# Splitting each mid-run K and V load into two half-row loads on two DMA queues

## The chip, the cores and the metric

The kernel runs on one core of a Trainium2 chip. The metric is the device time of one execution in microseconds (us). A core has a matrix engine (PE), a vector engine (VectorE, DVE in the profile), a scalar engine (ScalarE, ACT), GpSimd (POOL) and SyncE (SP), which only issues transfers, and 16 DMA engines that move data between the main memory (HBM) and the on-chip memory. Each engine runs its own list of instructions in order; they wait for each other by semaphores. A transfer is issued by an engine onto that engine's own DMA queue, and the 16 DMA engines work the queues off.

## The reference, cut to what matters

One decoding step of attention over a cache of 8192 positions, for 2 tokens (batch B = 2) and 32 heads of width 128, and a small MLP whose result gates the attention output. All arrays are float32.

```python
def _A_ref(x, k_cache, v_cache, wq, wo):      # x: 2 x 1 x 512, caches: 2 x 32 x 8192 x 128
    q = (x @ wq).reshape(B, Sq, H, Dh).transpose(0, 2, 1, 3)
    scores = jnp.einsum("bhqd,bhkd->bhqk", q, k_cache) * (Dh ** -0.5)
    p = softmax(scores, axis=-1)
    o = jnp.einsum("bhqk,bhkd->bhqd", p, v_cache)
    return o.transpose(0, 2, 1, 3).reshape(B, Sq, H * Dh) @ wo
def _B_ref(x, w1, b1, w2, b2):                # 512 -> 1376 -> 512
    return gelu(layernorm(x) @ w1 + b1) @ w2 + b2
xn = layernorm(A_x)
return A_x + _A_ref(xn, ...) * silu(_B_ref(xn, ...))
```

Every byte of the K and V caches (2 x 268 MB) has to be read once, and nearly all of the kernel's traffic is that.

## The kernel before, in words

The 64 (token, head) rows are handled two at a time, as N = 32 pairs. For one pair the 2 x 8192 keys lie over the 128 partitions, 64 partitions to a head, so that each partition holds 128 keys of 128 numbers: 16384 floats, 64 KB, in one row that is also contiguous in HBM. K of a pair is therefore one transfer of 128 rows of 64 KB (8.39 MB), and so is V. On the chip there are three such buffers: two for K (`kb0`, `kb1`, the K of alternate pairs) and one for V (`vb`).

What is done for pair n:

- VectorE multiplies K by the query in place, one half of the rows' length at a time (`scores_mul`, L523; half s = 0 is the first 64 keys of each partition, s = 1 the other 64), then sums each product (`scores_sum`, L530, again one instruction per half) and takes the maximum (L534), which PE turns (L537) and VectorE reduces (L540).
- In the next pair's time PE spreads the maximum (L546), ScalarE copies it (L547), takes the exponentials (L551) and scales a selector row (L555); this is `exps`.
- `weighted` is the product of the weights with V: 32 matmuls of 512 columns on PE (L574; the profile counts each as two instructions, hence x64), which read V from its first to its last column; ScalarE copies the result out (L581), PE folds it (L583) and VectorE places it (`spread`, L589).

The order is written out by hand. In the iteration of pair n VectorE runs mul(n, 0), the reduction of pair n-1, mul(n, 1), sum(n, 0), sum(n, 1), max(n) and spread(n-1); `exps` and `weighted` of pair n-1 lie beside them. `load_v(n)` is issued after `weighted(n-1)`, which frees `vb`; `load_k(n+2)` after the sums of pair n, which free that K buffer. All loads are issued by SyncE through `load` (L314), so they are on one queue in the order of the program. K of the first and of the last pair (n = 0 and 31) are already two loads of half a row each, both from SyncE; V of the last pair goes into `kb1` in the same way; then come five pieces of the output weights `wo` into `vb`.

`Plan` records every operation with the tiles that it reads and writes, and derives the waits from that: a load of a buffer waits for the last reader of it. In `emit` each engine's instructions come out in recorded order. Operations with `loop=True` (the middle pairs on PE, VectorE and ScalarE) are put into a hardware loop, for which each turn must have the same waits and the same signals; `HEADS` places the loop's head in the instruction buffer. SyncE has no loop: its loads are written out one by one. A PE instruction raises its semaphore only if somebody waits for it (`tell`).

Of the kernel before, what the change touches and what calls it, by code (L numbers as in the profile page):

```python
# [11 lines left out]

HEADS = {"pe": 0, "dve": 160, "act": 128}


class Op:
# [3 lines left out]
class Plan:  # L22
# [18 lines left out]
    def op(self, eng, fn, r=(), w=(), over=(), it=None, loop=False, dma=None):  # L41


        o = Op()
        o.eng, o.fn, o.it, o.loop, o.dma, o.tell = eng, fn, it, loop, dma, False
        need = {}

        def after(d, war):
            if d.dma is None and dma is None and d.eng == eng and (eng == "pe" or war):
                return  # L50
            if d.dma is None:
                if need.get(d.eng) is None or need[d.eng].idx < d.idx:
                    need[d.eng] = d
            else:
                k = ("dma", d.dma)
                if need.get(k) is None or need[k].idx < d.idx:
                    need[k] = d

        for k in r:
            if k in self.writer:  # L60
                after(self.writer[k], False)
        for k in list(w) + list(over):
            if k in self.writer:
                after(self.writer[k], False)
            for d in self.readers.get(k, ()):
                after(d, True)
        clock = self.clock[eng]
        need = {k: d for k, d in need.items() if clock.get(k, 0) < d.idx}
        o.deps = [(k, d) for k, d in need.items()
                  if not any(e is not d and e.done.get(k, 0) >= d.idx for e in need.values())]  # L70
        for _, d in o.deps:
            for k, v in d.done.items():
                clock[k] = max(clock.get(k, 0), v)
        own = eng if dma is None else ("dma", dma)
        self.count[own] = o.idx = self.count.get(own, 0) + 1
        o.done = dict(clock)
        o.done[own] = o.idx
        for k in w:
            self.writer[k] = o
            self.readers[k] = []  # L80
        for k in r:
            if k not in w:
                self.readers.setdefault(k, []).append(o)
        self.ops.append(o)

    def emit(self, heads):

        nc = self.nc
        for o in self.ops:
            for _, d in o.deps:  # L90
                d.tell = True
        sems, value, told = {}, {}, {}
        for o in self.ops:
            key = o.eng if o.dma is None else ("dma", o.dma)
            if key not in sems:
                sems[key] = nc.alloc_semaphore(o.eng if o.dma is None else f"dma_{o.dma}")

            step = 16 if o.dma is not None else int(o.tell or o.eng != "pe")
            told[key] = told.get(key, 0) + step
            value[id(o)] = told[key]  # L100
        for o in self.ops:
            o.waits = {k: value[id(d)] for k, d in o.deps}

        def put(o, waits, turn=None):
            e = self.eng[o.eng]
            for k, v in waits:
                e.wait_ge(sems[k], v)
            i = o.fn() if o.it is None else o.fn(o.it if turn is None else turn)
            if o.dma is not None:
                i.then_inc(sems[("dma", o.dma)], 16)  # L110
            elif o.tell or o.eng != "pe":
                i.then_inc(sems[o.eng], 1)

        def order(d):
            return sorted(d.items(), key=lambda kv: str(kv[0]))

        for e in self.eng:
            ops = [o for o in self.ops if o.eng == e]
            inside = [j for j, o in enumerate(ops) if o.loop]
            if not inside:  # L120
                for o in ops:
                    put(o, order(o.waits))
                if e == "sp":

                    nc.sync.wait_ge(sems[("dma", "out")], told[("dma", "out")])
                continue
            for o in ops[:inside[0]]:
                put(o, order(o.waits))
            turns = {}
            for j in inside:  # L130
                turns.setdefault(ops[j].it, []).append(ops[j])
            n, m = len(turns), len(turns[1])
            assert inside == list(range(inside[0], inside[-1] + 1)) and list(turns) == list(range(1, n + 1))
            assert all(len(t) == m for t in turns.values())


            body, ahead = [], {}
            for j in range(m):
                col = [turns[i][j] for i in range(1, n + 1)]
                assert len({o.tell for o in col[1:-1]}) == 1, j  # L140
                for o in col:
                    o.tell = col[1].tell
                ws = []
                for k in sorted(set().union(*(o.waits for o in col)), key=str):
                    if all(k not in o.waits for o in col[1:]):
                        ahead[k] = max(ahead.get(k, 0), col[0].waits[k])
                        continue
                    step = col[2].waits[k] - col[1].waits[k]
                    base = col[1].waits[k] - 2 * step
                    for o in col:  # L150
                        assert o.waits.get(k) == step * o.it + base or (o.it == 1 and k not in o.waits), \
                            (e, j, k, o.it, [x.waits.get(k) for x in col])
                    ws.append((k, step, base))
                body.append((col[1], ws))
            for k, v in order(ahead):
                self.eng[e].wait_ge(sems[k], v)
            et = self.eng[e].engine
            with nc.Fori(1, n + 1, 1, engines=bass.OrderedEngineSet([et]), head_slot={et: heads[e]}) as i:
                for o, ws in body:
                    put(o, [(k, i * step + base if base else i * step) for k, step, base in ws], i)  # L160
            for o in ops[inside[-1] + 1:]:
                put(o, order(o.waits))


def decode_kernel(nc, x, kc, vc, wq, wo, w1, b1, w2, b2, out):
# [13 lines left out]
    JW = 512 // DH  # L179
# [17 lines left out]
    op = plan.op  # L197
# [5 lines left out]
        op("dve", fn, r, w, it=it, loop=loop)  # L203

    def act(fn, r=(), w=(), it=None, loop=False):
        op("act", fn, r, w, it=it, loop=loop)

    def pool(fn, r=(), w=()):
        op("pool", fn, r, w)
# [10 lines left out]
    kb = [sbuf(f"kb{i}", [P, KP * DH]) for i in range(2)]  # L220
    vb = sbuf("vb", [P, KP * DH])
    kbuf = [t.rearrange("p (j d) -> p j d", d=DH) for t in kb]
    vbuf = vb.rearrange("p (j d) -> p j d", d=DH)
# [36 lines left out]
    boot = []  # L260
# [49 lines left out]
    vf = vc.rearrange("b h s d -> (b h s d)").rearrange("(n p j d) -> n p j d", p=P, j=KP, d=DH)  # L310
    M = KP // 2

    def load(dst, src, sem, w, over=()):
        op("sp", lambda: nc.sync.dma_start(dst, src), (), w, over=over, dma=sem)  # L314

    def load_k(n):
        i = (n + 1) % 2
        if n in (0, N - 1):
            for s in range(2):
                load(kbuf[i][:, s * M:(s + 1) * M], kf[n][:, s * M:(s + 1) * M], f"k{i}{s}", [("kb", i, s)])  # L320
            return
        load(kbuf[i], kf[n], f"kb{i}", [("kb", i, s) for s in range(2)])


    WO_PIECES = (0, 16, 24, 29, 31, 32)
# [175 lines left out]
    load_k(1)  # L501

    def load_v(n):
        load(vbuf, vf[n], "v", ["vb"], over=boot)

    load_v(0)

# [56 lines left out]
    def weighted(n):  # L564

        one = dict(it=n + 1, loop=n < N - 1)
        last = n == N - 1
        v = kbuf[1] if last else vbuf  # L570
        for t in range(NT):
            j = t % QT
            keys = [("kb", 1, t * JW // M)] if last else ["vb"]
            pe(lambda i, t=t, j=j, v=v: matmul(PO[R * j:R * j + U * JW, :], PZ[:, t].rearrange("p s j -> p (s j)"),  # L574
                                               v[:, t * JW:(t + 1) * JW, :].rearrange("p j d -> p (j d)"),
                                               start=(t < QT), stop=(t + QT >= NT)),
               keys + [("PZ", s) for s in range(U)], ["po"], **one)
        if last:
            busy(1)

        act(lambda i: nc.scalar.copy(O4, PO), ["po"], ["o4"], **one)  # L581
        for k in range(JW):
            pe(lambda i, k=k: matmul(PT[:, :U], O4[:, k * DH:(k + 1) * DH], mod[:, k:U * JW:JW],  # L583
                                     start=(k == 0), stop=(k == JW - 1)), ["o4", "mod"], ["s0"], **one)
# [32 lines left out]

    wo_r = wo.rearrange("(p c) n -> p c n", p=P)
    for i, (a, e) in enumerate(zip(WO_PIECES, WO_PIECES[1:])):
        load(wo_sb[:, a:e], wo_r[:, a:e], f"wo{i}", [("wo", i)], over=["vb"])  # L620

    max_dve(N - 1)
    exps(N - 1)
# [73 lines left out]
```

## Time and profile before

| | |
|---|---|
| Time, median of 3 runs | 1299.54 us (1299.47 to 1299.76) |
| Profiled execution, first to last instruction (span) | 1298.1 us; its own time is given by the span alone, and the median of the runs is 1.4 us above it |
| Busy share of DVE, PE, ACT | 87%, 31%, 6% |
| SyncE's queue q1 | 10936 packets, 559.36 MB, 99.7% of 16 DMA engines' span |
| Mean rate | 431 GB/s |

A packet is one piece that one DMA engine moves. "DMA share" in a table of stretches is the part of the 16 DMA engines' time in which a packet was in work. "SPq" marks the instruction with which SyncE issues a transfer. A row of the timeline gives the start in us, the duration in us, the engine, the line, the operation, output and input, how many, and in brackets the idle time just before and what ended it.

### The profile page before, as it was taken

What the parts mean: (1) busy time and instruction counts of PE and PEld (TensorE: products, weight loads), DVE (VectorE), ACT (ScalarE), POOL (GpSimd) and SP (SyncE); (2) the same over time, 40 slices, a digit from 0 to 9 for tenths busy, and PEclk for the clock granted to TensorE, in tenths of its full rate; (3) what the DMA queues carried; (4) which work ended last, traced back from release to release, by engine and by line L of the source; (5) the groups of instructions that cost most, each with busy time, mean ns of one, the idle gap of its engine ahead of it and who ended that gap; (6) DMA issues with size and microseconds to landing.
All of it is one profiled execution on the core that took longest, in us unless ns stands there. A gap on an engine that the chain in (4) does not pass through costs nothing.

```text
span 1298.1 us, 6788 instructions
## 1 busy us (share of the span) xinstructions
PE 408.0 (31%) x2728; PEld 123.3 (9%) x2728; DVE 1134.3 (87%) x276; ACT 77.7 (6%) x250; POOL 1.4 (0%) x8
## 2 busy tenths in 40 slices
PE   5603333312333312333321333321333321233327
PEld 1200111000101000101100101100001000001102
DVE  2499999988889988889988888988888988888991
ACT  1200000000000000000000000000000000000000
POOL 0000000000000000000000000000000000000000
PEclk9856666556666656666656666656666655666658
DMA  9999999999999999999999999999999999999998
GB/s 404 445 425 442 426 432 440 424 444 428 438 430 426 442 428 440 428 434 438 424 444 428 438 430 426 444 426 440 428 430 442 424 444 428 436 432 426 430 434 365
DMA packets 10943, 559.45 MB, mean 431 GB/s; under 512 B 1220, under 2 KB 1332, under 8 KB 1592
## 3 DMA queue, kind: packets, MB, share of 16 engines
q1 hardware_dynamic: 10936, 559.36, 99.7%
q8 instruction: 4, 0.07, 0.0%
q14 instruction: 3, 0.02, 0.0%
HBM read 559.30 MB, written 0.06 MB: 431 GB/s over the span
## 4 chain that ended last, share of the span: by engine, by line
DMA 68%; PE 24%; DVE 4%; issue 3%; ACT 0%; SPq 0%; DVEq 0%
DMA vb<-in_A_v_cache_dram 65%; PE po L574 21%; DMA vb<-in_A_wo_dram 2%; DVE sc L530 2%; DVE kb L523 1%; PE s L409 1%; DMA vb<-in_A_x_dram 1%; PE po L481 1%; PE s L451 0%; PE s L411 0%; PE acc L656 0%; DVE vb L417 0%; ACT L430 0%; PE s L458 0%; SPq L314 0%
## 5 line engine op out<-in xcount | busy, mean ns | idle before, releaser
L523 DVE TENSOR_TENSOR kb<-kb,Q 128x8192 f32<-128x8192 f32 x64 | 555.5, 8681 | 101.2 <-DMA kb<-in_A_k_cache_dram 91.9
L530 DVE TENSOR_REDUCE sc<-kb 128x64 f32<-128x8192 f32 x64 | 552.3, 8666 | 0.0
L574 PE MATMUL po<-vb,PZ 128*8 128x512 f32 x1984 | 284.4, 738 | 282.9 <-DMA vb<-in_A_v_cache_dram 280.3
L546 PE MATMUL s<-nm,srow 1*128 1x2 f32 x64 | 18.4, 355 | 360.0 <-DVE nm L540 360.0
L574 PEld LDWEIGHTS po<-vb,PZ 128*8 128x8 f32 x1984 | 56.8, 103 | 484.4 <-issue 481.6
L537 PE MATMUL s<-ident,mx 128*1 128x128 f32 x32 | 11.8, 369 | 198.9 <-DVE mx L534 198.9
L546 PEld LDWEIGHTS s<-nm,srow 1*128 1x128 f32 x64 | 15.7, 302 | 369.3 <-DVE nm L540 369.3
L581 ACT COPY o<-po 128x512 f32<-128x512 f32 x32 | 18.7, 585 | 527.5 <-PE po L574 527.5
L547 ACT COPY bias<-s 128x2 f32<-128x2 f32 x32 | 5.1, 160 | 624.0 <-PE s L546 624.0
L583 PE MATMUL s<-mod,o 128*128 128x2 f32 x256 | 33.6, 253 | 22.1 <-ACT o L581 22.1
L583 PEld LDWEIGHTS s<-mod,o 128*128 128x128 f32 x256 | 31.0, 191 | 51.4 <-ACT o L581 51.4
L551 ACT ACTIVATE PZ<-sc,bias 64x128 f32<-64x128 f32 x64 | 25.5, 399 | 1.8
L537 PEld LDWEIGHTS s<-ident,mx 128*1 128x1 f32 x32 | 2.5, 79 | 202.4 <-DVE mx L534 171.9
L589 DVE TENSOR_TENSOR Z<-blk,s 128x8 f32 (+1 forms) x32 | 5.2, 162 | 13.5 <-PE s L583 13.5
L417 DVE COPY vb<-vb 2x384 f32<-2x384 f32 x4 | 1.8, 500 | 15.6 <-ACT vb L413 15.6
L409 PE MATMUL s<-vb 128*2 128x512 f32 (+1 forms) x24 | 12.2, 658 | 0.3 <-ACT vb L374 0.3
L551 ACT ACTIVATION_READ_ACCUMULATOR PZ<-sc,bias 64x1 f32 x64 | 11.8, 185 | 0.0
L665 DVE TENSOR_TENSOR gate<-acc,gate 128x128 f32<-128x128 f32 x1 | 0.3, 291 | 12.1 <-PE acc L656 12.1
L574 PE MATMUL po<-kb,PZ 128*8 128x512 f32 x64 | 9.8, 779 | 1.4 <-ACT PZ L551 1.4
L534 DVE TENSOR_REDUCE mx<-sc 128x1 f32<-128x128 f32 x32 | 9.1, 286 | 1.1
L555 ACT ACTIVATE ZR<-half,rs 128x8 f32 (+1 forms) x32 | 9.6, 301 | 4.1
L540 DVE TENSOR_REDUCE nm<-s 1x2 f32<-1x128 f32 x32 | 8.7, 272 | 0.3 <-PE s L537 0.3
(88 smaller groups left out, 82.9 us busy)
## 6 DMA issues: line engine op xcount, KB each, us to landing
kb<-in_A_k_cache_dram SPq DMA_DIRECT2D x4, 4096.0 KB, 42.8
kb<-in_A_v_cache_dram SPq DMA_DIRECT2D x2, 4096.0 KB, 40.8
vb<-in_B_w_dram SPq DMA_DIRECT2D x2, 2752.0 KB, 12.6
vb<-in_A_wo_dram SPq DMA_DIRECT2D x1, 4096.0 KB, 20.6
vb<-in_A_wo_dram SPq DMA_DIRECT2D x1, 2048.0 KB, 25.1
vb<-in_A_wo_dram SPq DMA_DIRECT2D x1, 1280.0 KB, 27.7
vb<-in_A_wo_dram SPq DMA_DIRECT2D x1, 512.0 KB, 28.5
vb<-in_A_v_cache_dram SPq DMA_DIRECT2D x31, 29.3
```

What stands on the lines that cost most here:

```text
L409: pe(lambda f=f, w=w, ph=ph, c=c: matmul(ph[:B, :w], yT[:, c, :], w1_sb[:, c, f:f + w], start=(c == 0), stop=False), ["yT", "w1"], [k])
L481: pe(lambda i=i, c=c, wv=wv, a=a, j=j, hd=hd: matmul(PO[R * j:R * j + NQ * B, :].rearrange("m (h d) -> m h d", d=DH), xnT[:, c, a:a + NQ * ...
L523: vector(n, n, lambda n: nc.vector.tensor_tensor(out=k, in0=k, in1=cols(Q, n * DH, DH).unsqueeze(1).to_broadcast([P, M, DH]), op=ALU.mult) ...
L530: vector(n, n, lambda n: nc.vector.tensor_reduce(out=SC[:, s * M:(s + 1) * M], in_=k, axis=AX.X, op=ALU.add), [("kb", i, s)], [("sc", s)])
L534: vector(n, n, lambda n: nc.vector.tensor_reduce(out=MX, in_=SC, axis=AX.X, op=ALU.max), [("sc", 0), ("sc", 1)], ["mx"])
L537: pe(lambda i: transpose(PM[:1, :P], MX, ident), ["mx", "ident"], ["s1"], it=n, loop=n > 0)
L546: pe(lambda i: matmul(PN[:, :U], srow, NM, start=True, stop=True), ["srow", "nm"], ["s2"], **one)
L551: act(lambda i, r=r, s=s: nc.scalar.activation(PZ[r, :, s, :], sc[r], AF.Exp, bias=BIAS[r, s:s + 1], scale=SCALE, accum_out=RS[r]), ["bias ...
L555: act(lambda i: nc.scalar.activation(cols(ZR, i * UP - UP, UP), half, AF.Copy, scale=RS), ["half"] + [("rs", s) for s in range(U)], [("ZR" ...
L574: pe(lambda i, t=t, j=j, v=v: matmul(PO[R * j:R * j + U * JW, :], PZ[:, t].rearrange("p s j -> p (s j)"), v[:, t * JW:(t + 1) * JW, :].rea ...
L581: act(lambda i: nc.scalar.copy(O4, PO), ["po"], ["o4"], **one)
L583: pe(lambda i, k=k: matmul(PT[:, :U], O4[:, k * DH:(k + 1) * DH], mod[:, k:U * JW:JW], start=(k == 0), stop=(k == JW - 1)), ["o4", "mod"], ...
```

## The change

K of pairs 1 to 30 and V of pairs 0 to 30 are each loaded by two transfers of 128 rows of 32 KB in place of one of 128 rows of 64 KB. The first half of each row is issued by SyncE, the second by ScalarE (`q="act"`), each on its own queue and with its own semaphore. With that:

- The tile `vb` becomes two tiles, one for each half, so that the matmuls of the first 16 steps of `weighted` wait for SyncE's half alone, the others for ScalarE's; and each half of a buffer is loaded again when its own readers are done, no longer when the readers of the whole are.
- ScalarE's operations leave the hardware loop (`act` no longer hands on `loop`) and are written out one by one, 31 turns, since transfers are now among them. In ScalarE's order the load of V's half comes behind the copy L581, and the load of K's half behind that; the copy L547 of the next pair comes behind both.
- In `emit` the signals of the turns of a loop are made equal (`tell`), since a PE matmul in the middle of `weighted` now has somebody waiting for it.
- K of pairs 0 and 31, V of pair 31 and all other loads stay on SyncE.

```diff
-HEADS = {"pe": 0, "dve": 160, "act": 128}
+HEADS = {"pe": 0, "dve": 160}
...
+        for e in self.eng:
+            turns = {}
+            for o in self.ops:
+                if o.eng == e and o.loop:
+                    turns.setdefault(o.it, []).append(o)
+            for col in zip(*turns.values()):
+                said = any(o.tell for o in col)
+                for o in col:
+                    o.tell = said
...
     def act(fn, r=(), w=(), it=None, loop=False):
-        op("act", fn, r, w, it=it, loop=loop)
+        op("act", fn, r, w, it=it)
...
-    def load(dst, src, sem, w, over=()):
-        op("sp", lambda: nc.sync.dma_start(dst, src), (), w, over=over, dma=sem)
+    queue = {"sp": nc.sync, "act": nc.scalar}
+
+    def load(dst, src, sem, w, over=(), q="sp"):
+        op(q, lambda: queue[q].dma_start(dst, src), (), w, over=over, dma=sem)
...
-        load(kbuf[i], kf[n], f"kb{i}", [("kb", i, s) for s in range(2)])
+        for s, q in enumerate(("sp", "act")):
+            load(kbuf[i][:, s * M:(s + 1) * M], kf[n][:, s * M:(s + 1) * M], f"kb{i}{s}", [("kb", i, s)], q=q)
...
     def load_v(n):
-        load(vbuf, vf[n], "v", ["vb"], over=boot)
+        for s, q in enumerate(("sp", "act")):
+            load(vbuf[:, s * M:(s + 1) * M], vf[n][:, s * M:(s + 1) * M], f"v{s}", [("vb", s)], over=boot, q=q)
...
-            keys = [("kb", 1, t * JW // M)] if last else ["vb"]
+            keys = [("kb", 1, t * JW // M)] if last else [("vb", t * JW // M)]
...
-        load(wo_sb[:, a:e], wo_r[:, a:e], f"wo{i}", [("wo", i)], over=["vb"])
+        load(wo_sb[:, a:e], wo_r[:, a:e], f"wo{i}", [("wo", i)], over=[("vb", s) for s in range(2)])
```

## The prediction

> **What bounds the kernel now.** I read the page first: busy shares, the slices of DMA, the queues. Then the list of transfers.
>
> ```profile
> span 1298.1 us, 6788 instructions
> PE 408.0 (31%) x2728; PEld 123.3 (9%) x2728; DVE 1134.3 (87%) x276; ACT 77.7 (6%) x250; POOL 1.4 (0%) x8
> ...
> DMA  9999999999999999999999999999999999999998
> ...
> DMA packets 10943, 559.45 MB, mean 431 GB/s; under 512 B 1220, under 2 KB 1332, under 8 KB 1592
> ...
> q1 hardware_dynamic: 10936, 559.36, 99.7%
> q8 instruction: 4, 0.07, 0.0%
> q14 instruction: 3, 0.02, 0.0%
> ...
> vb<-in_A_v_cache_dram SPq DMA_DIRECT2D x31, 29.3
> kb<-in_A_k_cache_dram SPq DMA_DIRECT2D x30, 42.5
> ```
>
> The reader is to see that one queue, q1, keeps all 16 DMA engines at work for 99.7% of the span, with no weak slice. VectorE is next at 87%. So the time is the bytes over the rate of the DMA engines, and an edit counts only if it changes that rate, opens a gap in it, or lengthens what follows the last byte. The last two rows count the loads that the change touches: 31 + 30 = 61.
>
> Next, one pair in the middle from the timeline, to see how much hides behind the queue.
>
> ```profile
> 608.15 0.33 SPq L314 DMA_DIRECT2D vb<-in_A_v_cache_dram  x1
> 608.15 0.58 ACT L581 COPY o<-po 128x512 f32<-128x512 f32 x1 [18.00 <-PE po L574]
> 613.66 0.33 SPq L314 DMA_DIRECT2D kb<-in_A_k_cache_dram  x1
> 617.68 8.69 DVE L523 TENSOR_TENSOR kb<-kb,Q 128x8192 f32<-128x8192 f32 x1 [3.64 <-DMA kb<-in_A_k_cache_dram]
> 626.29 0.27 DVE L540 TENSOR_REDUCE nm<-s 1x2 f32<-1x128 f32 x1
> 627.24 0.16 ACT L547 COPY bias<-s 128x2 f32<-128x2 f32 x1 [18.50 <-PE s L546]
> 628.57 0.30 ACT L555 ACTIVATE ZR<-half,rs 128x8 f32 x1
> 635.09 17.26 DVE L530 TENSOR_REDUCE sc<-kb 128x64 f32<-128x8192 f32 x2
> 637.00 9.21 PE L574 MATMUL po<-vb,PZ 128*8 128x512 f32 x64 [9.80 <-DMA vb<-in_A_v_cache_dram]
> 656.36 8.69 DVE L523 TENSOR_TENSOR kb<-kb,Q 128x8192 f32<-128x8192 f32 x1 [3.58 <-DMA kb<-in_A_k_cache_dram]
> 665.17 8.67 DVE L523 TENSOR_TENSOR kb<-kb,Q 128x8192 f32<-128x8192 f32 x1
> ```
>
> Both readers wait for their transfer: VectorE 3.6 us in each pair, PE 9.8 us. A load is issued long before the queue gets to it: V is issued at 608.15, K of the pair before lands at 617.68 (9.5 us of work still ahead of it), V lands at 637.00.
>
> Last, the table of stretches, cut where PE starts on a new V, that is, where a V landed. The first two rows below, of the chain, mark two such starts; between them lie 27 pairs, (1217.52 - 172.57) / 27 = 38.70 us each. Columns of the stretches: length, busy time of each engine, granted PE clock, DMA share, GB/s.
>
> ```profile
> 172.57 9.37 PE po L574 x64
> ...
> 1217.52 9.14 PE po L574 x64
> ```
>
> ```profile
> 1101.41:1140.11 38.70, 11.12 (x75) 3.35 (x76) 35.09 (x8) 2.03 (x7) 0.00 (x0) 0.63 1.00 434
> 1178.83:1217.52 38.69, 11.66 (x76) 3.47 (x76) 35.08 (x8) 2.03 (x7) 0.00 (x0) 0.59 1.00 431
> 1217.52:1256.30 38.78, 11.10 (x76) 3.35 (x77) 38.71 (x8) 2.03 (x7) 0.00 (x0) 0.63 1.00 433
> 1256.30:1293.40 37.10, 30.81 (x211) 9.36 (x211) 12.87 (x8) 3.20 (x9) 0.00 (x0) 0.87 0.99 423
> ```
>
> The DMA share is 1.00 in each pair; a load of 8.39 MB costs 38.70 / 2 = 19.35 us, 433.5 GB/s.
>
> **The change, part by part.**
>
> *Twice as many packets, half as long.* Each of the 61 loads becomes two. The trace has this once: K of the last pair is already two loads of half a row, on the same queue (SyncE's row of two at 1188.92), and it moved in the stretch 1217.52 to 1256.30.
>
> ```profile
> 1188.92 5.61 SPq L314 DMA_DIRECT2D kb<-in_A_k_cache_dram  x2
> ```
>
> That stretch took 38.78 us where the others take 38.69 and 38.70, with a DMA share of 1.00, so nothing else held it up: 0.08 us more for one load in two halves. The rows scatter by some 0.02, so the price lies between 0.06 and 0.10. For 61 loads: 61 x 0.08 = 4.9 us (3.7 to 6.1), all on the path, since the DMA engines are the path.
>
> *Two queues at once.* No row shows two queues of loads side by side; the instruction queues q8 and q14, seven packets in all, are too small to tell. So this is bounded. Lower end: alternating queues hide what a packet costs by itself. Going from 64 KB to 32 KB rows doubled that cost and added 0.08 us per load, so the whole of it in a load of before is about 0.08 too; hidden, it would turn +4.9 into -4.9. Upper end: alternation costs more than the halving. The nearest row with a worse rate on mixed transfers is the last stretch, 423 GB/s; if the 61 loads ran at that, 61 x 19.35 = 1180 us would grow by 433.5/423 - 1 = 2.5%, +29.3 us. I take the halving's price unaltered (+0 for the second queue), because the row of K's halves is by far the nearest: same bytes, same row length, same engines, and DMA share 1.00 leaves no idle time that a second queue could fill.
>
> [...] The 0.33 us of SPq in the rows above already lies beside a full queue, so the trace agrees that there is nothing to save in issuing.
>
> *The loads on ScalarE's list.* V's second half is issued behind the copy L581, so 0.58 us later than before; the queue has 9.5 us of work then. Behind it stands the wait of K's second half, for sum(n, 1), which ends when K is issued in the rows (613.66). Queued behind that wait is L547, which cannot start before PE and L540 (627.24): 13 us of cover. Two issues of 0.33 us a pair end before that as well. `exps` ends at 628.87 and V lands at 637.00: 8 us more. Cost 0. If that cover were gone, PE would be late on V, and then the next load of V.
>
> *Earlier release.* V's first half is freed halfway through L574 (4.6 us earlier), K's first half after the first sum (8.6 us earlier). Neither queue can then run dry more easily than the one does now. Shared, each queue moves a K half and a V half per pair, and a half rides 19.35 us at half rate. V's second half needs 4.6 us of PE and 0.6 of copy between landing and the next issue, while the K half of its queue rides 19.35: 14 us of cover. K's halves are needed by the multiplies of two pairs on: from 613.66 to 665.17 for the second half, 51.5 us, against at most 38.7 of riding behind the V half. And if one queue is empty, the other alone can fill the engines, as q1 does now. Worth 0, cost 0: more margin where no wait sets the end.
>
> *Start.* ScalarE's first halves come behind its eight copies of the query.
>
> ```profile
> 50.82 0.43 SPq L314 DMA_DIRECT2D vb<-in_A_v_cache_dram  x1
> 58.22 0.59 ACT L496 COPY Q<-s 128x512 f32<-128x512 f32 x1 [0.27 <-PE s L494]
> 97.09 8.67 DVE L523 TENSOR_TENSOR kb<-kb,Q 128x8192 f32<-128x8192 f32 x1
> ```
>
> They are issued near 58.9, SyncE's two halves near 50.8; these are 8.39 MB, 19.35 us for the engines by themselves, so no gap opens. K's second half then lands some 20 us after 58.9, needed at 97.09. Cost 0.
>
> *ScalarE written out.* The loop body becomes 31 copies; with waits and issues some 15 instructions a pair. The page counts 0.07 MB in 4 packets on q8, some 17 KB each. I estimate the added code at two such packets; at one engine's share of the rate (433.5/16 = 27.1 GB/s) that is 0.6 us each, on one engine of 16, whose lag the last landing may show in full: 0 to 1.2, taken as 0.6 us. SyncE issues as many loads as before; PE gains one wait a pair, on a half that is there or lands with the other.
>
> *Sum.* 4.9 + 0 + 0.6 = +5.5 us on the span: 1298.1 becomes 1303.6. The median of the runs stands 1.4 above the span, so **1305.0 us**, 0.42% slower. 0.2% (2.6 us) is about what a measurement of this kernel can tell from no change.
>
> **The rivals.**
>
> 1. *The second queue hides the packets' cost (faster).* While one queue's packet ends, the other's is ready. For it: packets cost something by themselves, as the 38.78 shows. Against it: the share is 1.00 already. It decides from 0.13 hidden of the doubled cost of 0.16 us a load: (0.08 - 0.13) x 61 + 0.6 = -2.5 us. All hidden: -4.9 + 0.6, 1295.2; without the code's 0.6, 1294.6.
> [...]
>
> 2. *No change.* Alternation hides about the halving's addition and no more: 1299.5 to 1300.1. For it: half of the cost hidden is all it needs. Against it: the same as against rival 1.
> [...]
>
> 3. *Alternation costs more than the halving.* Place: each DMA engine, at each change of queue, 16 per load. Each 10 ns would be 61 x 16 x 0.01 = 9.8 us. Up to the bound above, 1298.1 + 29.3 + 1.4 = 1329. For it: it is the thing no row shows. Against it: nothing in the trace loses time between packets.
>
> 4. *The end comes late.* K of the last pair stays on SyncE whole, while V(30)'s second half rides beside it from about 1227. From 1217.52, 9.2 us alone move 4.0 MB, the other 4.4 MB at half rate take 20 us: landing near 1247.5.
>
> ```profile
> 1242.12 8.67 DVE L523 TENSOR_TENSOR kb<-kb,Q 128x8192 f32<-128x8192 f32 x1
> 1285.87 3.62 PE L647 MATMUL wide<-vb,on 128*2 128x512 f32 x32
> 1293.47 1.28 PE L656 MATMUL acc<-vb,on 128*2 128x128 f32 x40 [1.19 <-DMA vb<-in_A_wo_dram]
> ```
>
> The multiply would wait 5.4 us, and all behind it; L647 would start at 1291.3, where it has some 2.6 us to spare before the last weights: +2.8 us on top of my sum, 1307.8. Against it: SyncE's halves are released earlier than ScalarE's, so that queue is ahead by then. It decides if that lead is under some 5 us.
>
> **How the numbers follow.** My forecast, the halving's price alone, 0.45 (its own range 1302.2 to 1308); rival 3, 0.17; rival 4, 0.05; rival 2, 0.20; rival 1, 0.13. So faster 0.13, same 0.20, slower 0.67. The range takes in rival 1's bound and rival 3's: 1294.5 to 1329, leaving out about 1 in 10.
>
> **What would show it.** A second hardware queue with 61 x 144 = 8784 packets (128 rows and 16 completions a half) and 256 MB, q1 with as many packets as now and 303 MB; DMA slices at 9 throughout; a pair near 38.70 + 0.16 = 38.86 us; VectorE still waiting for K some 3 us a pair, or PE for V; L547 not later against L540; the last stretch, from the last V to the end, as long as now. A pair at 38.5 would show rival 1, one above 39 rival 3, a wait before the multiply at the end rival 4. The prediction is wrong if two queues share the engines in a way that one queue's rows cannot tell.

## The result, and the profile after

The changed kernel takes 1304.63 us (median of five runs, 1304.17 to 1304.80) against 1299.54: 5.1 us more, a ratio of 1.0039 with a 95% interval of 1.0027 to 1.0050. The profiled executions differ by 4.9 us, 1303.0 against 1298.1.

The page of the kernel after: busy shares, packets, queues (packets, MB, share of 16 DMA engines), and the row of VectorE's multiply. The last line by itself is that row in the kernel before.

```profile
span 1303.0 us, 6631 instructions
...
DMA  9999999999999999999999999999999999999998
...
DMA packets 19728, 559.46 MB, mean 429 GB/s; under 512 B 2196, under 2 KB 2308, under 8 KB 2568
...
q1 hardware_dynamic: 10936, 303.51, 54.2%
q10 hardware_dynamic: 8784, 255.86, 45.6%
...
L536 DVE TENSOR_TENSOR kb<-kb,Q 128x8192 f32<-128x8192 f32 x64 | 555.5, 8682 | 109.1 <-DMA kb<-in_A_k_cache_dram 99.8
```

```profile
L523 DVE TENSOR_TENSOR kb<-kb,Q 128x8192 f32<-128x8192 f32 x64 | 555.5, 8681 | 101.2 <-DMA kb<-in_A_k_cache_dram 91.9
```

The second queue is there, with 256 MB on it, and the DMA engines are as full as before (54.2 + 45.6 = 99.8%). The same bytes travel in nearly twice the packets, and the engines need longer for them. VectorE does the same work and waits a little more for K (99.8 us in place of 91.9). The table of stretches, one pair each, and two rows of the chain, 26 pairs apart, say where the time went:

```profile
596.92:635.79 38.87, 11.37 (x76) 3.35 (x77) 35.03 (x8) 2.03 (x7) 0.00 (x0) 0.63 1.00 432
1179.88:1218.75 38.87, 13.32 (x75) 3.62 (x76) 35.12 (x8) 2.03 (x7) 0.00 (x0) 0.63 1.00 432
```

```profile
177.85 5.36 PE po L587 x32
1188.23 5.36 PE po L587 x32
```

Single pairs take 38.87 us; on average over the 26 it is (1188.23 - 177.85) / 26 = 38.86 in place of 38.70, at a DMA share of 1.00 in both kernels: 0.16 us a pair, 0.08 for each load that is cut, and 61 x 0.08 = 4.9 us, the difference of the profiled executions. The loss is spread evenly over the run; there is no place where something stalls. Inside a pair (timeline, kernel after):

```profile
602.72 0.33 SPq L325 DMA_DIRECT2D vb<-in_A_v_cache_dram  x1
603.61 0.33 SPq L325 DMA_DIRECT2D kb<-in_A_k_cache_dram  x1
605.31 3.62 PE L587 MATMUL po<-vb,PZ 128*8 128x512 f32 x32 [2.65 <-DMA vb<-in_A_v_cache_dram]
609.00 0.33 ACTq L325 DMA_DIRECT2D vb<-in_A_v_cache_dram  x1
612.21 0.34 ACTq L325 DMA_DIRECT2D kb<-in_A_k_cache_dram  x1
616.39 8.69 DVE L536 TENSOR_TENSOR kb<-kb,Q 128x8192 f32<-128x8192 f32 x1 [3.80 <-DMA kb<-in_A_k_cache_dram]
625.00 0.27 DVE L553 TENSOR_REDUCE nm<-s 1x2 f32<-1x128 f32 x1
625.94 0.16 ACT L560 COPY bias<-s 128x2 f32<-128x2 f32 x1 [16.36 <-PE s L559]
635.79 5.08 PE L587 MATMUL po<-vb,PZ 128*8 128x512 f32 x32 [9.88 <-DMA vb<-in_A_v_cache_dram]
```

SyncE issues its half of K at 603.61, 8.6 us ahead of ScalarE's half (612.21): the earlier release works, and buys nothing, as both readers go on waiting for their transfers. ScalarE's loads hold nothing up: L560 follows L553 by 0.94 us, as L547 followed L540 before (626.29 to 627.24).

Only the end changed its face (timeline, kernel after, then the one row of the kernel before that answers to the last):

```profile
1249.02 8.69 DVE L536 TENSOR_TENSOR kb<-kb,Q 128x8192 f32<-128x8192 f32 x1 [5.68 <-DMA kb<-in_A_k_cache_dram]
1261.27 9.79 PE L587 MATMUL po<-vb,PZ 128*8 128x512 f32 x64 [17.29 <-DMA vb<-in_A_v_cache_dram]
1293.30 5.33 PE L660 MATMUL wide<-vb,on 128*2 128x512 f32 x48
1298.31 1.12 PEld L669 LDWEIGHTS acc<-vb,on 128*2 128x2 f32 x40 [0.61 <-DMA vb<-in_A_wo_dram]
1300.67 0.29 DVE L678 TENSOR_TENSOR gate<-acc,gate 128x128 f32<-128x128 f32 x1 [9.49 <-PE acc L669]
```

```profile
1295.83 0.29 DVE L665 TENSOR_TENSOR gate<-acc,gate 128x128 f32<-128x128 f32 x1 [12.08 <-PE acc L656]
```

The last K's second half is 5.68 us late for the multiply, and the output product starts at 1293.30, 7.4 us later than before (1285.87). It still meets the last weights just as they land (a wait of 0.61 us for them), and the multiplication by the gate behind it (L678, L665 before) is 4.84 us later than before: no more than what the transfers had lost by then.

### The profile page after: what moved, and what is told of

It is laid out like the page before. It is cut to its first block, busy times and chain, and to the rows that moved or that the text cites. A ratio compares the mean times of both kernels' runs of the same rounds, so it can differ in the third digit from the quotient of the medians.

```text
span 1303.0 us, 6631 instructions
## 1 busy us (share of the span) xinstructions
PE 432.5 (33%) x2728; PEld 125.3 (10%) x2728; DVE 1134.9 (87%) x276; ACT 77.7 (6%) x250; POOL 1.4 (0%) x8
## 2 busy tenths in 40 slices
DMA packets 19728, 559.46 MB, mean 429 GB/s; under 512 B 2196, under 2 KB 2308, under 8 KB 2568
## 3 DMA queue, kind: packets, MB, share of 16 engines
q1 hardware_dynamic: 10936, 303.51, 54.2%
q10 hardware_dynamic: 8784, 255.86, 45.6%
## 4 chain that ended last, share of the span: by engine, by line
DMA 74%; PE 15%; DVE 7%; issue 3%; another core or an unknown queue 1%; ACT 1%; DVEq 0%; SPq 0%
DMA vb<-in_A_v_cache_dram 74%; PE po L587 11%; DVE sc L543 3%; DVE kb L536 3%; PE s L421 1%; DMA vb<-in_A_x_dram 1%; PE po L493 1%; PE wide L660 0%; PE s L463 0%; PE s L574 0%; PE s L423 0%; ACT PZ L564 0%; PE s L596 0%; PE acc L669 0%
## 5 line engine op out<-in xcount | busy, mean ns | idle before, releaser
L536 DVE TENSOR_TENSOR kb<-kb,Q 128x8192 f32<-128x8192 f32 x64 | 555.5, 8682 | 109.1 <-DMA kb<-in_A_k_cache_dram 99.8
L587 PE MATMUL po<-vb,PZ 128*8 128x512 f32 x1984 | 312.7, 789 | 361.8 <-DMA vb<-in_A_v_cache_dram 359.2
L560 ACT COPY bias<-s 128x2 f32<-128x2 f32 x32 | 5.1, 160 | 526.2 <-PE s L559 526.2
L547 DVE TENSOR_REDUCE mx<-sc 128x1 f32<-128x128 f32 x32 | 9.2, 286 | 1.1
L568 ACT ACTIVATE ZR<-half,rs 128x8 f32<-128x8 f32 x32 | 9.6, 301 | 1.0
L553 DVE TENSOR_REDUCE nm<-s 1x2 f32<-1x128 f32 x32 | 8.7, 272 | 0.4 <-PE s L550 0.4
L678 DVE TENSOR_TENSOR gate<-acc,gate 128x128 f32<-128x128 f32 x1 | 0.3, 292 | 9.5 <-PE acc L669 9.5
```

What stands on the lines that cost most here:

```text
L536: vector(n, n, lambda n: nc.vector.tensor_tensor(out=k, in0=k, in1=cols(Q, n * DH, DH).unsqueeze(1).to_broadcast([P, M, DH]), op=ALU.mult) ...
L547: vector(n, n, lambda n: nc.vector.tensor_reduce(out=MX, in_=SC, axis=AX.X, op=ALU.max), [("sc", 0), ("sc", 1)], ["mx"])
L568: act(lambda i: nc.scalar.activation(cols(ZR, i * UP - UP, UP), half, AF.Copy, scale=RS), ["half"] + [("rs", s) for s in range(U)], [("ZR" ...
```

## The experiments

Two theories were set against each other. *Rows*: a packet costs a fixed time by itself, so cutting rows in half costs, on whatever queue. *Queues*: going to and fro between two queues costs, the length of the rows does not.

**One queue.**

```diff
-        for s, q in enumerate(("sp", "act")):
+        for s, q in enumerate(("sp", "sp")):
```

(in `load_k` and in `load_v`)

> The changed kernel with both halves of each load issued by SyncE: the same half rows, one queue. Theory rows (each packet costs a fixed time, whichever queue): 1304.6 us as with two queues, a pair 38.87 us. Rival queues (what costs is changing between two queues, the length of the rows nothing): back to 1299.5 us, a pair 38.70 us.

Measured: 1304.15 us (1303.95 to 1304.41), ratio 1.0035 (1.0021 to 1.0049), span 1303.0, as in the changed kernel. Its page and its timeline, two starts of PE on a new V:

```profile
q1 hardware_dynamic: 19720, 559.36, 99.8%
```

```profile
1173.86 5.42 PE L587 MATMUL po<-vb,PZ 128*8 128x512 f32 x32 [9.87 <-DMA vb<-in_A_v_cache_dram]
1212.73 6.46 PE L587 MATMUL po<-vb,PZ 128*8 128x512 f32 x32 [9.90 <-DMA vb<-in_A_v_cache_dram]
```

1212.73 - 1173.86 = 38.87 us, as in the stretches of the changed kernel. The packet records that the traces keep (start, length, size and queue of each packet) say the same. They name no engine, but by their times they fall into 16 sequences in which one packet begins as another ends. In those of the changed kernel, from 200 to 1100 us, 87% of the data packets follow one of the other queue, and a 32 KB packet takes 1213.6 ns on average, from its start to the start of the next; on one queue it takes 1213.6 as well. The second queue has no price and no worth; all of the loss is in the cut. *Queues* falls.

**Quarters.** Each half row issued as two quarter rows, two on each queue.

```diff
-        for s, q in enumerate(("sp", "act")):
-            load(vbuf[:, s * M:(s + 1) * M], vf[n][:, s * M:(s + 1) * M], f"v{s}", [("vb", s)], over=boot, q=q)
+        for s in range(4):
+            load(vbuf[:, s * M // 2:(s + 1) * M // 2], vf[n][:, s * M // 2:(s + 1) * M // 2], f"v{s}", [("vb", s)], over=boot,
+                 q=("sp", "act")[s // 2])
```

(K likewise, with the readers' tiles to match)

> The changed kernel with each half row issued as two quarter rows (16 KB), two on each queue. Theory rows: a load has 24 packets more per DMA engine than before in place of 8, so three times the loss, +14.7 us, 1314.2 us, a pair 39.19 us. Rival queues: twice the changes of queue of the changed kernel, +9.8 us, 1309.4 us.

Measured: 1314.45 us (1313.98 to 1315.15), ratio 1.0115 (1.0099 to 1.0130). The starts on a V's second quarter, two pairs apart (timeline):

```profile
1108.05 5.91 PE L589 MATMUL po<-vb,PZ 128*8 128x512 f32 x32 [4.69 <-DMA vb<-in_A_v_cache_dram]
1186.36 6.02 PE L589 MATMUL po<-vb,PZ 128*8 128x512 f32 x32 [4.16 <-DMA vb<-in_A_v_cache_dram]
```

78.31 / 2 = 39.16 us a pair. The loss of 15.0 us is three times that of the halves (5.1), as *rows* had it: 0.08 us for the first cut of a load, (39.16 - 38.70) / 2 / 3 = 0.08 for the mean of three. Each of these cuts adds a transfer too, so the run can't tell packets from transfers; the next two try that.

**The row cut, the transfer not.** A cut adds packets, and it adds a transfer with its completions (2196 packets under 512 B in the changed kernel against 1220 before: 16 for each of 61). Naming the row as two runs in one load was to separate them:

```diff
-        load(kbuf[i], kf[n], f"kb{i}", [("kb", i, s) for s in range(2)])
+        load(kbuf[i].rearrange("p (s j) d -> p s (j d)", s=2), kf[n].rearrange("p (s j) d -> p s (j d)", s=2),
+             f"kb{i}", [("kb", i, s) for s in range(2)])
```

(in the kernel before; V likewise)

> The kernel before, one queue and one load of each K and V, but each row named as two runs of 32 KB. If the two runs become two packets, theory rows: about 1304 us, as the packets are those of the changed kernel and only the completions fewer. Rival (the second transfer and its completion cost, not the packets): 1299.5 us. If the runs are joined again into packets of 64 KB, 1299.5 us and the run says nothing.

Measured: 1299.42 us, ratio 1.0000 (0.9991 to 1.0009). The page has the packets of before, so the runs were joined and this says nothing:

```profile
DMA packets 10943, 559.45 MB, mean 431 GB/s; under 512 B 1220, under 2 KB 1332, under 8 KB 1592
```

So the runs were kept apart by 64 bytes of room between the halves in each K buffer:

```diff
-    kb = [sbuf(f"kb{i}", [P, KP * DH]) for i in range(2)]
+    GAP = 16
+    kb = [sbuf(f"kb{i}", [P, KP * DH + 2 * GAP]) for i in range(2)]
...
-    kbuf = [t.rearrange("p (j d) -> p j d", d=DH) for t in kb]
+    kbuf = [t.rearrange("p (s x) -> p s x", s=2)[:, :, :KP * DH // 2] for t in kb]
```

(the rest of the edit lets loads and readers use the two halves)

> The kernel before, one queue and one load of each K and V, but with 64 bytes of room in each K buffer between the two halves of a row, so that a row of the 30 middle K loads cannot be joined into one packet of 64 KB and becomes two of 32 KB. No transfer and no completion is added. Theory rows: 30 of the 61 loads pay for 8 more packets per DMA engine, 30 x 0.08 = 2.4 us less the completions, so +2.1 to +2.4, 1301.6 to 1301.9 us. Rival (the second transfer with its completion is what costs): 1299.5 us.

Measured: 1301.04 us (1300.82 to 1301.24) against 1299.37, ratio 1.0013 (1.0004 to 1.0022). The page, and a stretch of four pairs:

```profile
DMA packets 14783, 559.45 MB, mean 430 GB/s; under 512 B 1220, under 2 KB 1332, under 8 KB 1592
```

```profile
1025.39:1180.41 155.02, 44.72 (x300) 13.55 (x301) 140.25 (x29) 8.11 (x28) 0.00 (x0) 0.61 1.00 433
```

3840 packets more (30 x 128), as many completions as before (1220 under 512 B). A pair, with one cut load in it, takes 155.02 / 4 = 38.755 us: 0.055 for the cut of the rows alone, 30 x 0.055 = 1.7 us, and 1.67 was measured. That is less than I expected. So of the 0.08 us two thirds are the packets, 0.055 / 8 = 7 ns for each packet more on a DMA engine; the rest, some 0.025, comes with the second transfer.

The packet records bear this out. From its start to the start of the next on its engine, a packet of 64 KB takes 2418.1 ns on average in the kernel before, one of 32 KB takes 1212.5 in this run and 1213.6 in the changed kernel, and the 4 bytes of a completion, of which each engine has one per transfer, take 5.9. For one load that is 16 x 1212.5 - 8 x 2418.1 = 55 ns for the rows alone, 6 for the second completion, and 16 x 1.0 = some 16 because the same 32 KB packets are slower when the halves are two transfers: 0.077 us in all. Why they are slower is open.

**ScalarE written out, alone.**

```diff
-HEADS = {"pe": 0, "dve": 160, "act": 128}
+HEADS = {"pe": 0, "dve": 160}
...
-        op("act", fn, r, w, it=it, loop=loop)
+        op("act", fn, r, w, it=it)
```

> The kernel before with ScalarE's operations written out and nothing else changed. The prediction's term for the longer code: 1299.5 to 1300.7 us. Rival code (the written-out list is what costs): near 1304.6 us.

Measured: 1299.46 us (1299.38 to 1299.80) against 1299.47, ratio 1.0000 (0.9991 to 1.0009). The longer list is free.

**Whole rows on two queues: K by SyncE, V by ScalarE.**

```diff
-        for s, q in enumerate(("sp", "act")):
-            load(kbuf[i][:, s * M:(s + 1) * M], kf[n][:, s * M:(s + 1) * M], f"kb{i}{s}", [("kb", i, s)], q=q)
+        load(kbuf[i], kf[n], f"kb{i}", [("kb", i, s) for s in range(2)])
...
-            load(vbuf[:, s * M:(s + 1) * M], vf[n][:, s * M:(s + 1) * M], f"v{s}", [("vb", s)], over=boot, q=q)
+        load(vbuf, vf[n], "v", [("vb", s) for s in range(2)], over=boot, q="act")
```

> The changed kernel with whole rows of 64 KB again, but K issued by SyncE and V by ScalarE, so two queues run side by side. Theory rows: no packet more than before, so 1299.5 to 1300.1 us, a pair 38.70 us. Rival queues: half as many changes of queue as with half rows, so about half of the loss, 1302 us, a pair 38.78 us.

Measured: 1445.88 us, ratio 1.1136 (1.1110 to 1.1162). Both theories missed by far, and the run can't judge them, since the DMA engines were not kept busy. Timeline and one stretch:

```profile
622.57 8.32 PE L585 MATMUL po<-vb,PZ 128*8 128x512 f32 x64 [18.83 <-DMA vb<-in_A_v_cache_dram]
630.97 0.33 ACTq L325 DMA_DIRECT2D vb<-in_A_v_cache_dram  x1
670.05 8.47 PE L585 MATMUL po<-vb,PZ 128*8 128x512 f32 x64 [27.54 <-DMA vb<-in_A_v_cache_dram]
678.60 0.34 ACTq L325 DMA_DIRECT2D vb<-in_A_v_cache_dram  x1
```

```profile
620.00:670.05 50.05, 10.09 (x76) 3.25 (x77) 44.29 (x10) 2.03 (x7) 0.00 (x0) 0.60 0.84 356
```

V now shares the engines with K and needs 39.1 us from issue to use (630.97 to 670.05) where it needed 28.9 on the single queue (608.15 to 637.00). With PE's pass over the one V buffer that makes a round of 678.60 - 630.97 = 47.6 us, longer than the 38.70 that the bytes need; when K's two buffers are full and V has landed, nothing is left to move, and the share falls to 0.84 (0.62 from 610.00 to 630.90). The queue's order had been worth something: K waited while V went at full rate (in 19.3 us, from 617.68 to 637.00). In the changed kernel each queue carries half of both, and the share stays at 1.00; that this is what saves it was not tested.

**Halves by partitions.**

```diff
-            load(vbuf[:, s * M:(s + 1) * M], vf[n][:, s * M:(s + 1) * M], f"v{s}", [("vb", s)], over=boot, q=q)
+            load(vbuf[HP * s:HP * (s + 1)], vf[n][HP * s:HP * (s + 1)], f"v{s}", [("vb", s)], over=boot, q=q)
```

(K likewise; the readers wait for both halves)

> The changed kernel with each load cut by partitions in place of along the row: 64 rows of 64 KB by SyncE, 64 by ScalarE, at the same time. Two transfers on two queues per load as in the change, but no row is shorter. Theory rows: as many data packets as before, only 16 completions of some bytes more per load: 1299.5 to 1300.7 us. Rival queues: 1302 us or more. A third way: if each half of the partitions keeps only part of the DMA engines busy, time is lost whenever the two queues are out of step, and it is far slower.

Measured: 2485.93 us, ratio 1.9017 (1.8973 to 1.9061): far slower, as the third way had it, though its reason, engines left idle, is not what the page shows. From the list of queues, and two starts on a V from the timeline:

```profile
DMA  9999999999999999999999999999999999999998
GB/s 393 219 217 219 219 216 209 219 218 219 218 217 217 213 215 218 219 219 218 217 213 215 217 218 219 215 217 210 219 218 216 216 213 216 217 217 218 212 269 319
DMA packets 11921, 559.46 MB, mean 225 GB/s; under 512 B 2197, under 2 KB 2309, under 8 KB 2569
...
q1 hardware_dynamic: 7032, 303.51, 52.4%
q10 hardware_dynamic: 4880, 255.86, 47.5%
```

```profile
608.28 8.33 PE L588 MATMUL po<-vb,PZ 128*8 128x512 f32 x64 [29.18 <-DMA vb<-in_A_v_cache_dram]
685.65 8.89 PE L588 MATMUL po<-vb,PZ 128*8 128x512 f32 x64 [29.18 <-DMA vb<-in_A_v_cache_dram]
```

A pair takes 77.37 us, twice 38.70, at half the rate (217 GB/s), with every DMA engine "busy" (52.4 + 47.5 = 99.9%): a full row of DMA shows that packets are in work, not that they move at full speed. The packet records add what the engines did: from 300 to 2300 us, in 73% of the time 14 or more of the 16 engines had a packet of the same queue in work, so of the same half of the partitions, and a packet of 64 KB took 4.85 us on average, where it took 2.42 in the kernel before. Why the engines keep step in this way is not shown. For the theories the run says nothing.

**The end on two queues.**

```diff
-                load(kbuf[i][:, s * M:(s + 1) * M], kf[n][:, s * M:(s + 1) * M], f"k{i}{s}", [("kb", i, s)])
+                load(kbuf[i][:, s * M:(s + 1) * M], kf[n][:, s * M:(s + 1) * M], f"k{i}{s}", [("kb", i, s)],
+                     q=("sp", "act")[s if n else 0])
```

(and the last V in the same way)

> The changed kernel with the halves of the last K and of the last V on the two queues as well. VectorE's wait of 5.7 us for the last K's second half at the end should be gone. Theory rows: the end is set by the bytes and their packets, that wait is hidden by the last weights, so 1304.6 us. Rival end (part of the 4.9 us comes from the late last K): 1302 to 1303 us.

Measured: 1305.74 us (1304.58 to 1308.32), ratio 1.0055 (1.0042 to 1.0068), span 1303.0. Timeline, then a piece of the chain that ended last:

```profile
1247.89 8.69 DVE L537 TENSOR_TENSOR kb<-kb,Q 128x8192 f32<-128x8192 f32 x1 [1.86 <-DMA kb<-in_A_k_cache_dram]
```

```profile
1235.49 48.80 DMA kb<-in_A_v_cache_dram
```

The wait shrank from 5.68 to 1.86 us and nothing was gained. But the last V's second half now lands late instead (1235.49 + 48.80 = 1284.3), so this run by itself doesn't clear the late K. The run on one queue does (its timeline):

```profile
1241.78 8.69 DVE L536 TENSOR_TENSOR kb<-kb,Q 128x8192 f32<-128x8192 f32 x1 [0.84 <-DMA kb<-in_A_k_cache_dram]
1298.38 1.28 PE L669 MATMUL acc<-vb,on 128*2 128x128 f32 x40 [1.19 <-DMA vb<-in_A_wo_dram]
```

There the last K is late by 0.84 us alone, PE waits 1.19 us for the last weights as in the kernel before, and the multiplication by the gate comes no sooner (it starts at 1300.71 against 1300.67 in the changed kernel): the late last K was no part of the loss. The runs with the end on two queues scatter more (1304.58 to 1308.32 us) than those of any other kernel with half rows; why is open.

**End pairs whole.**

```diff
-        if n in (0, N - 1):
-            for s in range(2):
-                load(kbuf[i][:, s * M:(s + 1) * M], kf[n][:, s * M:(s + 1) * M], f"k{i}{s}", [("kb", i, s)])
-            return
```

> The kernel before with K of the first and of the last pair in one load each, so two loads fewer in halves. Theory rows: 2 x 0.08 = 0.16 us less of DMA time, 1299.3 us, if nothing else is late. Rival end: VectorE gets the last K some 3.6 us later (near 1236.9 in place of 1233.3), and what follows it, not the last weights, sets the end: 1299.5 to 1302 us.

Measured: 1302.23 us (1301.17 to 1303.24), ratio 1.0023 (1.0013 to 1.0032), span 1300.1 against 1298.1 in the kernel before. VectorE's first multiply from the chains, this run's and then that of the kernel before; then this run's timeline:

```profile
56.41 17.29 DVE kb L519 x2
```

```profile
52.90 17.29 DVE kb L523 x2
```

```profile
1238.17 8.69 DVE L519 TENSOR_TENSOR kb<-kb,Q 128x8192 f32<-128x8192 f32 x1 [3.51 <-DMA kb<-in_A_k_cache_dram]
1257.63 9.70 PE L570 MATMUL po<-vb,PZ 128*8 128x512 f32 x64 [9.94 <-DMA vb<-in_A_v_cache_dram]
1290.36 5.33 PE L643 MATMUL wide<-vb,on 128*2 128x512 f32 x48
```

The loss begins at the start: VectorE gets the first K 3.5 us later, and the last V that goes into `vb` lands at 1257.63 in place of 1256.30, so 1.3 of the 2.0 us by which the span grew lie ahead of the end. There VectorE waits 3.51 us for the last K where it found it ready before, and the output product runs its 48 steps in one go without a wait for weights, so what follows the last K has become as late as the weights. The halves that the kernel before has at its two ends together more than pay for their packets; how much each end is worth by itself was not run. In the middle both readers wait for transfers anyway, and there the halves only cost. No version tried is faster than the kernel before.

## Why the prediction was right

Forecast 1305.0 us, measured 1304.63. The mechanism, dearer transfers on a path that the DMA engines set, is what the runs show. That the second queue adds nothing was taken from the nearest row, not worked out, and the forecast gave itself 0.45; the run on one queue is what shows it. The range, 1294.5 to 1329, would have held most other outcomes too.

- *Packets, +4.9 us.* Right in size and cause: +0.16 us a pair (38.86, as forecast), the same on one queue, three times as much for quarters. What the step called the cost of packets is two thirds packets and one third the second transfer; the row it was read from held both, so the sum didn't suffer. That one row (38.78) was enough is borne out by the 61 loads, at 0.08 each.
- *Two queues, 0.* Right: one queue and two give the same pair (38.87 us), and packets of the same length to 0.1 ns (1213.6). So rivals 1 and 3, which both needed an effect of alternating, and rival 2, which needed it to pay for the halving, are out. Issuing from two engines saved nothing: 1304.15 us on one queue and 1304.63 on two; the loss came from the cut that it took to use the second.
- *ScalarE written out, +0.6 us.* Wrong by its whole size: 0.0 measured, and q8, from whose packets the term was estimated, moved 4 packets after as before. Without it the sum is +4.9 us on the span, which is what was measured. So the forecast is 0.4 us off because the term is missing (-0.6) and the medians of the runs differ by 0.2 more than the spans (5.1), for which no run shows a reason.
- *ScalarE's loads and the earlier release, 0.* Right, by the rows of the pair above.
- *Rival 4.* Its wait came (5.68 us, worked out as 5.4), but not its price: the weights were 4.9 us later too, so the product met them without loss (what follows it is 4.84 later). The step there set the late chain against the weights' old landing time.
- *Packets and queues* are as forecast: 8784 packets and 256 MB on the new queue, q1 with 10936 packets and 303 MB.

## What to carry to other kernels

When the table of stretches shows a DMA share of 1.00 at the best rate that the trace has (434 GB/s in steady stretches here; the share alone is not enough, as the halves by partitions show), a second queue has nothing to fill (1304.15 us here on one, 1304.63 on two); look instead at what a change does to the packets, and price it from any load in the trace that is already cut that way. A cut can pay where one reader's wait delays all that follows (the ends of this kernel, 2.9 us for both) and costs where the transfers are the path throughout (0.08 us a load here). Two queues also give up the order of one: with whole rows, V then shared the engines with K and took 39.1 us in place of 28.9.

## What the runs showed of the hardware

- A packet of 32 KB against half of one of 64 KB cost about 7 ns more on its DMA engine (0.055 us a load of 8 more packets each), in transfers as large as 8.39 MB; a completion took 6 ns of its engine.
- Two queues at once were served packet by packet in turn on each engine (87% of the packets followed one of the other queue), at no price: 1213.6 ns for each 32 KB packet on two queues and on one.
- Loads cut by partitions, 64 and 64 on two queues, ran at 217 GB/s in place of 433.5 while every DMA engine counted as busy (52.4 + 47.5 = 99.9%).
- The list of 31 turns written out on ScalarE cost nothing (1299.46 against 1299.47 us).
